# A new order of the same steps in a state read followed by a mixture of attention experts

## The chip, the cores and the metric

One core of a Trainium2 chip runs the whole program. The metric is the device time in microseconds, the median of several executions. The engines are named as in the profile: PE is TensorE (matmuls; PEld are its weight loads), DVE is VectorE, ACT is ScalarE, POOL is GpSimd, SP is SyncE, which issues all DMAs of this kernel.

## What is computed

There are two stages, for 8 batches (B) of 8 heads (H), 512 tokens (S), 32 states (Ns) and 64 features (D). First, tokens read states and states read tokens:

```python
scores = scale * np.matmul(x, state.transpose(0, 1, 3, 2))
a = softmax(scores); xread = np.matmul(a, state)
scores2 = scale * np.matmul(state, x.transpose(0, 1, 3, 2))
a2 = softmax(scores2); sread = np.matmul(a2, x)
x = concat([xread, sread], axis=2)      # then (B, 544, 512)
```

(`softmax` and `concat` stand here for the lines of the reference that spell them out.) Then the 544 rows of each batch, 512 features wide, go through four experts of causal attention with 64 features each. The logits `x @ w_gate` choose two experts for each row; q, k and v are projected by each expert's weights, the masked softmax of q k^T is applied to v, the result goes through the expert's `wo`, and each row's two experts are added with their gate weights. The weights of q and k are 200 times larger than drawn.

## The kernel before

Most products are made in f16 with each operand split in two parts: the high part is a cast to f16, the low part is the f16 of what the cast left over, and three products (high by high, high by low, low by high) are added in PSUM. Batch 0 is done in f32 and batch 1 partly. So nearly every tensor has a step that makes the high part (a cast, on ACT, POOL or DVE) and one that makes the low part (a subtraction, on DVE or POOL).

For each batch b, `front(b)` (line 744; `first`, line 660, for batch 0) loads x into the tile `xn` (one buffer only), splits it into `xh` (`parts_of_x`, line 610), transposes it by DMA into `xT`, makes the scores against the state (`bd`), their softmax in `eb` (`row_softmax`, line 633), its transpose `at`, the weights folded with the state `gs`, and from `at` and `gs` the values `v`, the keys `kt` and the masked queries `qf`, which are split into `qh` and transposed by DMA into `qm`. `side(b)` (line 856) makes the states' own read (`e2`, `a2`, `a2t`, `rd`, `xt_tail`). `gate` (line 881) makes the gate weights in a chain of small DVE and ACT steps. `probs(b, i)` (line 920) makes the attention scores of query tile i (128 rows), their softmax in a `p32` tile (named p in the profile), splits it into `ph` and sends it by DMA transpose to `pt`. `reads(b, i)` (line 990) multiplies `pt` by `v`, scales the result into `z32` (named z), adds its two shared quarters (a step of its own that DVE or POOL can do), splits it into `zh` and transposes it into `z`; `outs` (line 1030) multiplies by `wo_n` and stores `o`. `tail` (line 1045) does the 32 state rows of each pair of batches. `load_wo` (line 568) loads wo in two pieces and splits them into `wo_n` (`hi_lo`, line 446, whose low part is made by `low`, line 433).

Nothing is issued while these functions run: each operation is recorded as a step with a number, its possible engines ("ways") and the buffers that it touches. `Steps.run` (line 346) then issues the 2022 steps in the order of a text written out by hand, `ORDER`. An entry is the step's number, a dot, and the number of the way: for the low part made by `low` way 0 is DVE and way 1 is POOL (two instructions there, a scaling and a subtraction); for an addition on z32 way 0 is POOL and way 1 is DVE; for a cast made by `split` (line 425) way 0 is ACT, 1 is POOL and 2 is DVE. A third number puts that many extra matmuls before the step. So the text sets the order of every engine's queue, SP's queue of DMA issues among them. The dictionary `SLOTS` gives, for each tag with several buffers, which buffer each new use takes, in the order of the text: `bank` are the eight banks of PSUM, for example.

```python
for entry in order:
    s = self.all[int(entry[0])]
    calls = s["ways"][int(entry[1])][2]
    for b in s["bufs"].values():
        if b.slot is None:
            b.slot = self.tags[b.tag][int(next(left[b.tag])) if b.tag in left else 0]
```

All instructions of the steps carry line 362 in the profile, so one tells them apart by tiles. The steps that the prediction names: 265 and 283 are the additions on z32 of two query tiles of batch 0; 266 is a cast of zh; 205 is the low part of the second half of `wo_n`; 589 are the scores of batch 2's x against its state; 398 is a projection of batch 1 (keys, in f32).

Of the kernel before, what the change touches and what calls it, by code (L numbers as in the profile page):

```python
# [125 lines left out]
    "mb": "11000101",  # L126
    "sbm": "01011010",
    "bd": "0101010",
    "m2": "00110010",
    "gs1": "0101010101010",  # L130
    "kt": "010201020",
    "lg": "0100011010010",
# [1076 lines left out]
```

## Time and profile before

| | us |
|---|---|
| median of 3 runs | 285.36 |
| the runs | 285.03, 285.36, 286.33 |
| the profiled execution | 285.13 |
| its span, first to last instruction | 283.1 |
| PE busy in it | 270.6 |
| DVE busy | 240.1 |
| ACT busy | 216.2 |
| POOL busy | 202.6 |
| mean granted clock of TensorE | 0.994 |

The span is 2.0 us shorter than the profiled execution's own time; that rest lies around the first and last instruction. A matmul's end is modelled and matmuls are pipelined, so a high busy share of PE says that matmuls follow one another closely, not that the array is full. The granted clock is a share of 2.4 GHz.

### The profile page before, as it was taken

What the parts mean: (1) busy time and instruction counts of PE and PEld (TensorE: products, weight loads), DVE (VectorE), ACT (ScalarE), POOL (GpSimd) and SP (SyncE); (2) the same over time, 40 slices, a digit from 0 to 9 for tenths busy, and PEclk for the clock granted to TensorE, in tenths of its full rate; (3) what the DMA queues carried; (4) which work ended last, traced back from release to release, by engine and by line L of the source; (5) the groups of instructions that cost most, each with busy time, mean ns of one, the idle gap of its engine ahead of it and who ended that gap; (6) DMA issues with size and microseconds to landing.
All of it is one profiled execution on the core that took longest, in us unless ns stands there. A gap on an engine that the chain in (4) does not pass through costs nothing.

```text
span 283.1 us, 9753 instructions
## 1 busy us (share of the span) xinstructions
PE 270.6 (96%) x3659; PEld 182.7 (65%) x3660; DVE 240.1 (85%) x772; ACT 216.2 (76%) x713; POOL 202.6 (72%) x267
## 2 busy tenths in 40 slices
PE   8997999699999999897999999999999999999994
PEld 4956657277566755677657576776656757676752
DVE  2779999989999999999899989989899768878530
ACT  3768899389897998687989899847996755766643
POOL 7736966689796997866997899967896755438200
PEclk9999999899999999999999999999999999999999
DMA  7959869999999999999999999999957987899845
GB/s 197 186 167 136 215 158 181 239 176 145 195 250 205 191 203 243 200 194 243 205 183 211 182 243 247 229 222 182 133 122 140 153 151 95 134 238 210 158 167 186
DMA packets 154575, 53.20 MB, mean 188 GB/s; under 512 B 140576, under 2 KB 150048, under 8 KB 154528
## 3 DMA queue, kind: packets, MB, share of 16 engines
q1 hardware_dynamic: 154528, 52.59, 97.5%
q8 instruction: 28, 0.46, 0.7%
q14 instruction: 19, 0.16, 0.2%
HBM read 11.02 MB, written 8.91 MB: 70 GB/s over the span
## 4 chain that ended last, share of the span: by engine, by line
PE 60%; DVE 18%; POOL 9%; DMA 5%; issue 3%; ACT 2%; SPq 0%; POOLq 0%; ACTq 0%; DVEq 0%
PE bank L362 60%; DVE xh L362 4%; DMA xn<-in_x_dram 4%; POOL ph L362 2%; POOL eb L362 2%; DVE z L362 2%; DVE bank L362 2%; DMA pt<-ph 1%; POOL qh L362 1%; POOL a L362 1%; DVE v L362 1%; POOL at L362 1%; DVE qh L362 1%; DVE ph L362 1%; DVE qf L362 1%
## 5 line engine op out<-in xcount | busy, mean ns | idle before, releaser
L362 PE MATMUL bank<-gs,at 128*128 128x260 f16 (+3 forms) x352 | 52.3, 294 | 1.7 <-ACT at L362 1.4
L362 PE MATMUL bank<-kt,qm 128*128 128x128 f16 (+13 forms) x368 | 47.7, 313 | 0.0
L362 PE MATMUL bank<-wo_n,z 128*128 128x512 f16 (+1 forms) x198 | 46.1, 373 | 0.0
L362 PE MATMUL bank<-v,pt 128*128 128x192 f16 x480 | 44.1, 246 | 0.8 <-DMA pt<-ph 0.5
L362 PEld LDWEIGHTS <-pt 128*128 128x128 f16 x480 | 40.0, 98 | 4.2 <-DMA pt<-ph 2.3
L362 POOL TENSOR_TENSOR ph<-p,ph 128x256 f16<-128x256 f32 (+3 forms) x25 | 34.0, 1365 | 4.3 <-ACT ph L362 2.4
L362 DVE CUSTOM_DVE_ANT_0 bank<-bank,causal 128x128 f32<-128x128 f32 (+3 forms) x64 | 30.5, 502 | 5.5 <-PE bank L362 4.8
L362 ACT ACTIVATE p<-bank,mx 128x128 f32<-128x128 f32 (+3 forms) x64 | 33.3, 524 | 0.9
L362 PEld LDWEIGHTS <-at 128*128 128x128 f16 x288 | 27.5, 97 | 6.2
L362 PEld LDWEIGHTS <-qm 128*128 128x128 f16 (+1 forms) x336 | 20.2, 96 | 16.0 <-issue 5.6
L362 PEld LDWEIGHTS <-z 128*128 128x128 f16 x198 | 18.8, 98 | 18.1 <-issue 0.7
L362 PE MATMUL bank<-at,gs 128*128 128x512 f16 (+2 forms) x96 | 26.7, 413 | 1.6 <-DVE v L362 1.6
L362 ACT ACTIVATE o<-bank 128x512 f32<-128x512 f32 (+1 forms) x35 | 20.4, 583 | 6.8 <-PE bank L362 6.7
L362 DVE SCALAR_TENSOR_TENSOR xh<-xn,xh 128x512 f16<-128x512 f32 x24 | 20.4, 865 | 5.1 <-ACT xh L362 5.1
L362 ACT ACTIVATE xh<-xn 128x512 f16<-128x512 f32 x32 | 19.3, 624 | 6.2 <-DMA xn<-in_x_dram 6.2
L362 POOL TENSOR_TENSOR zh<-z,zh 128x256 f16<-128x256 f32 x25 | 18.6, 751 | 7.5 <-ACT zh L362 6.3
L362 POOL TENSOR_TENSOR qh<-qf,qh 128x384 f16<-128x384 f32 x21 | 19.9, 956 | 2.5 <-ACT qh L362 2.3
L362 POOL TENSOR_SCALAR ph<-p 128x256 f16<-128x256 f32 (+3 forms) x15 | 12.1, 810 | 12.5 <-ACT p L362 12.3
L362 DVE TENSOR_TENSOR z<-bank,c 128x384 f32<-128x384 f32 x32 | 17.3, 546 | 3.2 <-PE bank L362 2.0
L362 POOL TENSOR_TENSOR a<-e,a 128x512 f16<-128x512 f32 x15 | 18.3, 1223 | 1.0 <-ACT a L362 0.8
L362 POOL TENSOR_TENSOR z<-z 128x128 f32<-128x128 f32 x23 | 10.6, 466 | 10.7 <-DVE z L362 10.4
L362 POOL TENSOR_TENSOR eb<-eb,sbm 128x512 f32<-128x512 f32 x13 | 14.4, 1109 | 5.3 <-DVE sbm L362 5.3
(213 smaller groups left out, 648.6 us busy)
## 6 DMA issues: line engine op xcount, KB each, us to landing
out_dram<-o SPq DMA_DIRECT2D x33, 256.0 KB, 2.8
xn<-in_x_dram SPq DMA_DIRECT2D x14, 512.0 KB, 5.1
xn<-in_x_dram SPq DMA_DIRECT2D x4, 256.0 KB, 3.8
sn<-in_state_dram SPq DMA_DIRECT2D x8, 64.0 KB, 3.6
p<-in_moe_wo_dram SPq DMA_DIRECT2D x2, 256.0 KB, 3.5
xT<-xh SPq DMA_TRANSPOSE x28, 4.0
pt<-ph SPq DMA_TRANSPOSE x25, 4.5
p<-in_moe_wv_dram SPq DMA_DIRECT2D x1, 384.0 KB
```

The source lines that it names most:

```text
L362: f(**{k: v.ap() if isinstance(v, View) else v for k, v in kw.items()})
```

## The change

Only `ORDER` and `SLOTS` differ; the steps and the code that records them stay. All lines of both are replaced. Compared entry by entry, the same 2022 steps stand in both orders. 98 of them have another way:

| from, to | steps |
|---|---|
| ACT to DVE | 18 |
| ACT to POOL | 18 |
| DVE to ACT | 17 |
| DVE to POOL | 18 |
| POOL to ACT | 8 |
| POOL to DVE | 19 |

A step's place in the text moves by 9 places in the mean, by 205 at most (a step of a constant's mask). On TensorE the order of the steps is the same but for some twelve short stretches; of SP's 172 issues 125 can be left in their old order. The two stretches of the text around the steps 265 and 283, in full lines:

```diff
-263.0 786.0 421.0 282.0 264.0 273.0 365.0 369.0 275.0 261.1 581.1 426.0 372.0 360.0 265.1 283.1 21.0 373.0 361.0 376.0 401.0 362.0 366.0 582.0 589.0
-371.0 276.0 380.0 377.0 381.0 378.0 379.0 382.0 204.0 205.1 367.0 278.1 383.0 363.0 384.0 609.0 385.1 597.0 608.0 590.0 610.0 386.0 596.0 284.0 266.0
...
+263.0 281.0 372.0 282.0 366.0 260.0 367.0 585.0 264.0 274.0 273.0 360.0 373.0 362.0 361.0 370.0 369.0 376.0 205.0 261.1 414.0 401.0 581.1 582.0 589.0
+275.0 426.0 265.0 283.0 266.1 276.0 371.0 380.0 377.0 381.0 378.0 363.0 379.0 284.0 382.0 398.0 374.0 609.0 597.0 608.0 590.0 278.1 383.0 596.0 384.0
...
```

Here 261 is the low part of one ph tile (on DVE, way 1, in both), 276 that of a larger one (on POOL in both), 371, 367, 363 and 375 are evictions of the low part of v on DVE, and 277 (in the next line of the text) is the DMA transpose of the ph tile that 276 completes.

The line that holds the load of wo's second half (step 203), and the one with the first half of batch 5's x (1266), before and after:

```diff
-329.1 330.0 422.0 345.0 215.0 233.0 344.0 234.0 346.0 337.1 423.0 235.0 118.0 338.0 240.0 241.0 355.0 356.0 203.0 571.0 218.0 573.0 1053.0 424.0
-816.0 549.0 817.0 903.0 839.0 1062.0 688.0 836.0 489.0 833.0 1266.0 907.0 904.0 831.0 834.0 824.1 703.0 704.0 837.0 825.0 1265.0 493.0 826.0 490.0
...
+321.0 322.0 314.0 197.1 324.0 131.0 318.0 132.0 315.0 84.0 180.0 108.0 81.0 85.0 319.0 325.0 194.0 316.0 207.0 86.0 160.0 137.0 203.0 570.0 88.0
+709.0 718.0 719.0 722.1 552.0 723.0 1074.1 499.0 1266.0 553.0 554.0 725.0 726.0 504.0 710.1 505.0 828.1 829.0 740.0 741.0 711.0 720.0 721.0 1075.0
...
```

`SLOTS` changes with it, tag by tag; three of its lines:

```diff
-    "xh": "3021031203210312",
-    "p32": "12020101010212102110210212001201201002102",
-    "mb": "11000101",
...
+    "xh": "0123013210230123",
+    "p32": "01210202020120120120102102112101120121102",
+    "mb": "01011001",
...
```

## Rows read from the trace of the kernel before

**Rows 1.** Busy us (x instructions) of PE, PEld, DVE, ACT, POOL by stage, clock, DMA
```profile
20.20:57.70 37.50, 33.35 (x394) 21.17 (x396) 35.77 (x117) 30.31 (x102) 26.41 (x30) 0.95 0.90 184
57.70:128.40 70.70, 69.22 (x1036) 46.59 (x1024) 67.61 (x211) 61.11 (x204) 57.91 (x65) 1.00 1.14 201
128.40:278.60 150.20, 148.37 (x2045) 101.25 (x2040) 124.34 (x424) 112.33 (x383) 104.98 (x123) 1.00 0.96 183
```

**Rows 2.** Pieces of the chain that ended last: start us, us, what
```profile
106.59 4.46 DMA xn<-in_x_dram
...
221.50 57.91 PE bank L362 x716
```

**Rows 3.** DVE's timeline, 47.9 to 54.2 us: start, us, engine, line, operation, tiles
```profile
49.43 2.42 DVE L362 TENSOR_TENSOR z<-z 128x128 f32<-128x128 f32 x2
51.77 0.41 DVE L362 SCALAR_TENSOR_TENSOR v<-bank,v 128x256 f16<-128x256 f32 x1
...
53.19 0.41 DVE L362 SCALAR_TENSOR_TENSOR v<-bank,v 128x256 f16<-128x256 f32 x1
```

**Rows 4.** POOL's timeline in the same stretch; in brackets the idle time before
```profile
49.53 2.16 POOL L362 TENSOR_TENSOR ph<-p,ph 128x1024 f16<-128x1024 f32 x1 [0.98 <-ACT bank L362]
```

**Rows 5.** PE's timeline, 43 to 58 us
```profile
51.26 0.84 PE L362 MATMUL bank<-xT,bd 64*32 64x512 f16 x24 [0.87 <-ACT v L362]
53.66 3.18 PE L362 MATMUL bank<-at,gs 128*128 128x512 f32 x4 [1.55 <-DVE v L362]
```

**Rows 6.** Busy times around the half clock, and in another poor stretch
```profile
49.50:54.30 4.80, 2.38 (x31) 1.15 (x30) 4.66 (x14) 1.79 (x9) 2.31 (x2) 1.00 0.95 221
54.30:57.70 3.40, 3.40 (x76) 1.39 (x78) 3.40 (x10) 1.50 (x6) 3.32 (x5) 0.50 1.20 278
21.20:28.30 7.10, 5.48 (x24) 4.51 (x25) 6.89 (x28) 5.95 (x25) 4.57 (x7) 1.00 0.92 136
```

**Rows 7.** Groups by shape: count, busy us, mean ns, idle before
```profile
L362 POOL TENSOR_TENSOR z<-z 128x128 f32<-128x128 f32 x23 | 10.6, 466 | 10.7 <-DVE z L362 10.4 <-DVE gt L362 0.3
L362 DVE TENSOR_TENSOR rd<-bank,s 128x128 f32<-128x128 f32 x8 | 2.2, 279 | 0.7 <-ACT sums L362 0.3 <-PE bank L362 0.2
L362 DVE SCALAR_TENSOR_TENSOR xh<-xn,xh 128x512 f16<-128x512 f32 x24 | 20.4, 865 | 5.1 <-ACT xh L362 5.1
L362 DVE SCALAR_TENSOR_TENSOR gs<-bank,gs 128x512 f16<-128x512 f32 x12 | 8.0, 666 | 0.2 <-ACT gs L362 0.2
L362 DVE SCALAR_TENSOR_TENSOR v<-bank,v 128x256 f16<-128x256 f32 x32 | 13.1, 416 | 0.0
```

**Rows 8.** DVE's timeline, two low parts of xh that took long
```profile
114.49 1.59 DVE L362 SCALAR_TENSOR_TENSOR xh<-xn,xh 128x512 f16<-128x512 f32 x1
...
123.12 2.08 DVE L362 SCALAR_TENSOR_TENSOR xh<-xn,xh 128x512 f16<-128x512 f32 x2
```

**Rows 9.** SP's timeline, the first transposes of x
```profile
21.66 5.81 SPq L362 DMA_TRANSPOSE xT<-xh  x4
```

**Rows 10.** Busy times by stage again, 188 to 218 us
```profile
188.40:203.40 15.00, 15.00 (x222) 10.17 (x220) 14.01 (x40) 11.36 (x35) 12.27 (x15) 1.00 1.08 201
203.40:218.40 15.00, 15.00 (x239) 9.23 (x239) 13.20 (x45) 12.67 (x46) 12.55 (x13) 1.00 0.56 115
```

**Rows 11.** Groups by shape, POOL's casts and subtractions
```profile
L362 POOL TENSOR_SCALAR qh<-qf 128x384 f16<-128x384 f32 x4 | 2.4, 606 | 1.8 <-DVE qf L362 1.8
L362 POOL TENSOR_SCALAR at<-et 128x512 f16<-128x512 f32 x2 | 1.5, 753 | 1.1 <-PE bank L362 1.1
L362 POOL TENSOR_SCALAR ph<-p 128x768 f16<-128x768 f32 x3 | 3.7, 1231 | 5.8 <-ACT p L362 5.8
L362 POOL TENSOR_SCALAR a<-e 128x512 f16<-128x512 f32 x5 | 3.5, 690 | 1.2 <-ACT e L362 1.2
L362 POOL TENSOR_TENSOR qh<-qf,qh 128x384 f16<-128x384 f32 x21 | 19.9, 956 | 2.5 <-ACT qh L362 2.3 <-ACT wgt L362 0.2
L362 POOL TENSOR_TENSOR at<-et,at 128x512 f16<-128x512 f32 x9 | 10.4, 1160 | 3.5 <-ACT at L362 3.4
```

More of the change, by code (lines that the diff above doesn't have):

```diff
@@ L29 @@
 ORDER = """
[89 rows of a table removed]
[89 rows of a table added]
 """
 SLOTS = {
-    "bank": ("012347621350472631417326747026401256017137025702317513265023470126571564150326024176421046021564315025470241027360457602"
-          "431720465237164052341765765403153672410365201647521047251054321576040361245307631275764305712476123406243104505631256147"
-          "20356172461502364752167325016357430261573542650361275643217254675173246012320174662467130175046073157632"),
-    "xh": "3021031203210312",
-    "p32": "12020101010212102110210212001201201002102",
-    "mb": "11000101",
-    "sbm": "01011010",
-    "bd": "0101010",
[L129 to L132, printed above, removed]
-    "s2": "10101010",
-    "gt1": "0111010100011",
-    "a2": "1011101010101010",
-    "gs2": "1010110101001",
-    "gw": "0101110101010",
-    "m6": "11101010",
-    "a2t": "01011101",
-    "qf": "01001001010101101010100110100101",
-    "wgt": "01010101",
-    "qm": "00101101",
-    "mx": "31333212030102310203312031203121",
-    "sums": "01001010",
-    "ph": "0122011202102102011010120",
-    "xt_tail": "0010",
-    "c6": "0011010101010101",
-    "z32": "02100120102010211021210221021120",
-    "zh": "001110101010101",
-    "z": "111010010110101111",
-    "qh": "01101010010110",
-    "o": "1203122023101303213022310102312013",
-    "tw2": "0101",
-    "m4": "0101",
-    "twg": "0101",
-    "tmt": "0101",
-    "tmx": "1100",
-    "tsm": "1101",
-    "tpt": "0100",
-    "tc4": "1000",
-    "tz": "01",
@@ new lines @@
+    "bank": ("210374625103461752672465241531251370236146327623146714760235650341754657652135704257340273240637106426745245027605320176"
+          "451372604715304726410350453214763041273625340172354103721420640735251452067431052411760537142312456051364156757230417612"
+          "54037125627354026135074153076514265173041625740136204563205724507431270362134167002736405132046351205647"),
+    "xh": "0123013210230123",
+    "p32": "01210202020120120120102102112101120121102",
+    "mb": "01011001",
@@ new lines @@
+    "sbm": "00011010",
+    "m2": "01011100",
+    "bd": "0101010",
+    "kt": "012021021",
+    "lg": "0101101000011",
+    "s2": "01010101",
+    "gs1": "0101110101101",
+    "a2": "0101010110100101",
+    "gt1": "1010100000001",
+    "gs2": "1010101101010",
+    "gw": "0101101001001",
+    "a2t": "01011001",
+    "m6": "11101010",
+    "qf": "01010101010110010101010101010110",
+    "qm": "01110011",
+    "wgt": "10110101",
+    "mx": "20133021130102310312031203313210",
+    "sums": "01010101",
@@ L162 @@
+    "ph": "0100120012201202102120120",
+    "xt_tail": "1010",
+    "c6": "0110101010010101",
+    "z32": "12022012011221012102101201200120",
+    "zh": "011010110100101",
+    "z": "010001100101011001",
+    "qh": "10100110010101",
+    "o": "0120323102313212302100132032313012",
+    "tw2": "0100",
+    "m4": "0111",
+    "twg": "1010",
+    "tmt": "1101",
+    "tmx": "1010",
+    "tsm": "0100",
+    "tpt": "0010",
+    "tc4": "0101",
+    "tz": "10",
 }
```

170 rows, old and new, of the table ORDER are left out of this document.

## The prediction

> **What bounds the kernel now.** I read busy time by stage first, then the chain of waits, then the timeline of the place where DVE looks worst, then the groups of instructions by shape. From 128.4 us to 278.6 us TensorE is busy 148.37 of 150.20 us at full clock [rows 1], and the chain's last long piece is 57.91 us of matmuls [rows 2]. Nothing but fewer matmuls would shorten that stage, and the change removes none. So what the change is worth must be earned before 128.4 us, as an earlier start of that stage. In the two stages before it TensorE idles 37.50 - 33.35 = 4.2 us and 70.70 - 69.22 = 1.5 us, and DVE is nearly full: 35.77 of 37.50 us, then 67.61 of 70.70 us [rows 1]. DVE is what the matmuls run against there.
>
> The dearest place is 49 to 58 us. Two DVE additions on the z rows (steps 265 and 283, 128 elements each) take 2.42 us together [rows 3]; an operation of that size with one operand in PSUM takes 0.28 us [rows 7]. In the same time POOL subtracts the low half of a ph tile, from 49.53 to 51.69 us [rows 4], and the second addition ends 0.16 us behind it. So DVE stood still for some 1.9 us (2.42 less twice 0.28). Behind it in DVE's queue are the evictions of v at 51.77 and 53.19 us [rows 3], and the first projection matmul that waits for one (step 398) starts at 53.66 us, released by a DVE v [rows 5]. From 54.30 us the granted clock is 0.50, the 1.2 GHz level, for 3.40 us; before that TensorE was busy 2.38 of 4.80 us [rows 6]. In another poor stretch, 5.48 of 7.10 us, the clock stayed at 1.00 [rows 6].
>
> **The change, part by part.** The diff keeps all 2022 steps; 98 of them change engine, 25 of these before 128.4 us, and the rest is order and buffers.
>
> *The two additions go to POOL* (265.1 and 283.1 become .0). DVE loses 2.42 us. POOL gains two additions of 0.466 us [rows 7] about where it idles 0.98 us before its ph subtraction [rows 4]; that subtraction and the transpose behind it come up to 0.9 us later, which the loads of x that stand ahead of that transpose in SP's queue cover (without them the reads of pt would come 0.9 us later). A cast of zh (step 266) goes to POOL as well, behind the same cover. In exchange the low half of wo_n (step 205) comes to DVE: 0.67 us without a stall, 0.87 us as pieces of that size with both operands in SBUF average [rows 7]. DVE net: 2.42 - 0.67 = 1.75 us earlier. The bounds are 2.4 us (wo_n fits a gap) and -0.9 us (the subtractions of wo_n and ph, which DVE now runs there, wait behind a POOL step as the addition did, up to 2.16 us, and 0.67 us is added). I take 1.75, since POOL's long subtraction stands behind the additions in the new order and DVE's pieces ahead of it.
>
> *TensorE at that place.* Step 398 gets another PSUM bank, whose last reader is the v eviction of 51.77 us and not that of 53.19 us. By DVE's 1.75 us this eviction ends near 50.4 us. What is late next is step 589, the scores, which waits for transposes of x whose place in SP's queue stays: it starts at 51.26 and takes 0.84 us [rows 5] (the trace names ACT as its releaser, long done by then, so I read a transpose). So 398 starts at about 52.1 us, 1.5 us earlier; bounds 0 and 3.2 us. The 3.40 us at half clock did 1.7 us of work: worth 0 or 1.7 us, and with the shorter wait before it I take 1.7. TensorE then leads by 3.2 us at 57.7 us, but DVE only by 1.75, and DVE is the fuller engine from there [rows 1]: the smaller number passes on.
>
> *DVE's other engine changes before 128.4 us.* Between 20 and 50 us a low part of wn and a copy of kt leave DVE, 256 elements each, 0.42 us by the eviction of that size [rows 7], and a few small scalings come: 0.5 us less. Between 57.7 and 128.4 us a subtraction of zh and a cast of a2 leave (some 0.42 us each) and one of qh comes: by the same rows 0.3 us less, or 0.7 us with the stall that zh had; I take 0.5. These lie on a nearly full engine and I count them whole: 1.0 us, bounds 0 and 1.4.
>
> *The other stalls.* A low part of xh, both operands in SBUF, averages 865 ns on DVE; the same operation from PSUM takes 666 ns [rows 7]. So 24 x 0.2 = 4.8 us are lost in the kernel as above, and two places of the full stage show it: 1.59 - 0.67 = 0.9 us, and 2.08 - 1.33 = 0.75 us for a pair [rows 8]. By my count in the order DVE has 62 steps of over 0.3 us with both operands in SBUF before, and 60 after. They may fall better or worse by some 2.5 us, half of the 4.8; I take 0.
>
> The rule behind it: the Trainium skill (SBUF — State Buffer, SBUF: two separate sides) says that a DVE operation with two SBUF inputs and a GpSimd operation that reads SBUF take an exclusive lock on a shared port pair, so that the later one waits for the whole of the other. The 2.42 us agree. The rule also speaks against the change: the low parts of wo_n and ph on DVE would wait whole for the POOL steps that now stand beside them, and by it alone the gain at this place could be nothing; that is the first rival.
>
> *SP's queue.* 47 of its 172 issues change places. The load of wo's second half (step 203, 256 KB) goes ahead of the four transposes of x at 21.66 us [rows 9], where SP is idle before them; at the 184 GB/s of that stage [rows 1] it needs 1.4 us, between the landing of x and those transposes: 0, at worst 1.4 us, and I take 0. Stores of o go ahead of some transposes, and the first half of batch 5's x now goes out right before the second: 0 where SP waits for data anyway, up to 1.5 us (three stores of some 0.5 us) where it does not; I take 0, and the rest stands in the second rival.
>
> *After 128.4 us.* 73 of the engine changes lie here, on engines with slack while TensorE is full: nothing, as long as that slack lasts (the last rival). [...]
>
> **Sum.** 1.75 + 1.0 + 0.2 = 2.95 us, say 3.0. The profiled execution took 285.13 us, 0.23 us under the median of 285.36; against the median this gives 282.4 us, 1.1% faster. A measurement of this kernel can tell about 0.5%, 1.4 us, from no change.
>
> **Rivals.** *The lock forms again* at 49 to 54 us: the 1.75 us are not won, and wo_n's 0.67 us is paid. For it speaks the rule, and POOL's 2.16 us; against it the order, which places DVE's pieces first. Of the rest 1.2 - 0.7 = 0.5 us stays: 284.9 us.
>
> *The lead is eaten between 57.7 and 128.4 us.* The chain goes through a landing of x, 4.46 us from 106.59 us [rows 2]. Both halves of that load now stand together, where one went out earlier, so that 1 MB and not 0.5 MB has to land behind the second, and SP has less slack. Against it: POOL's work ahead of it loses a qh subtraction, 0.956 us [rows 11]. Of the 3.0 us only what lies behind is kept, some 0.7 us: 284.7 us.
>
> *More stalls vanish.* Those of rows 8 and their like do not recur, 2.5 us: 279.9 us. For it: the two come from chance neighbours; against it: as many such steps remain.
>
> *Slower: POOL fills up at 188 to 218 us.* It is busy 12.27 and 12.55 of 15.00 us there [rows 10]. Four casts come to it (qh 0.606, at 0.753 twice, ph 1.231 us), one leaves (a2 0.690), two subtractions come (qh 0.956, at 1.160) and one addition leaves (0.466) [rows 7, 11]: 4.3 us onto 5.2 us of idle time. TensorE gets pt and qm through POOL and SP. It decides from the point at which stalls take the remaining 0.9 us; then TensorE waits up to 4.3 us, and with a stretch at half clock like that above 1.7 us more: 285.36 - 3.0 + 4.3 to 6.0 = 286.7 to 288.4 us. Against it: most of the 4.3 us lies at the end of that stretch, and a transpose that comes late there has to use up TensorE's lead over it first.
>
> **How the numbers follow.** Forecast 0.42 (280.9 to 283.9 us by its own unknowns), more stalls vanish 0.17, lock again 0.10, lead eaten 0.14, POOL 0.17. The range is 278.8 to 287.4 us: it leaves out the far halves of the two outer cases, about 0.17. Faster by over 0.5% (under 283.9 us): 0.41 + 0.17 = 0.58. Within 0.5%: 0.01 + 0.24 x 0.8 = 0.20. Slower (over 286.8 us): the POOL case and what the two middle rivals cost when they come together, 0.17 + 0.05 = 0.22.
>
> **What would show it.** Right: the z additions on POOL at 0.47 us; no half clock near 54 us; the v evictions near 50 us; the stage of full TensorE starting about 3 us earlier and taking 150 us as before. Wrong: a DVE subtraction of 1.5 us or more at 49 to 54 us; a lead at 58 us that is gone by 128 us; TensorE idle for more than 3 us after 128 us; POOL busy over 14.5 of 15 us with SP waiting for it.

## The result: 0.7% slower, and the profile after

The changed kernel takes 288.03 us (median of 14 runs, 286.67 to 288.97) against 285.63 us for the kernel before (14 runs, 284.01 to 287.80): a ratio of 1.0072, 95% interval 1.0046 to 1.0098. The forecast was 282.4 us, 278.8 to 287.4. It lies outside, on the other side of the kernel before.

Busy times of the changed kernel by the stages of [rows 1], same columns (us, busy us of PE, PEld, DVE, ACT, POOL, granted clock, DMA share, GB/s):

```profile
20.20:57.70 37.50, 35.95 (x432) 23.57 (x431) 35.97 (x126) 32.27 (x108) 29.53 (x37) 1.00 0.91 176
57.70:128.40 70.70, 65.69 (x1014) 43.91 (x1014) 64.10 (x201) 59.07 (x197) 56.82 (x63) 1.00 1.11 202
128.40:278.60 150.20, 146.09 (x2017) 99.51 (x2002) 125.31 (x426) 101.64 (x360) 107.35 (x129) 1.00 1.00 180
```

Up to 57.7 us TensorE did more (35.95 us busy, not 33.35), and the half clock is gone. Behind it TensorE, no longer full, idles 5.0 us and 4.1 us, where it idled 1.5 and 1.8 us [rows 1]. DVE is no fuller than before (64.10 of 70.70 us). So TensorE now waits for something else. The table of waits, PE alone, from 57 to 280 us (us in total, times, longest), first of the kernel before:

```profile
PE bank L362 <- DVE qf L362: 1.6, 1, 1.6
PE bank L362 <- DVE kt L362: 0.7, 1, 0.7
PE bank L362 <- DMA pt<-ph: 0.5, 1, 0.5
...
```

and of the changed kernel:

```profile
PE bank L362 <- DMA qm<-qh: 5.1, 5, 1.8
PE bank L362 <- DMA pt<-ph: 2.0, 2, 1.3
PE bank L362 <- issue: 0.9, 1, 0.9
PE bank L362 <- DMA z<-zh: 0.4, 1, 0.4
...
```

That is the result in one view: 9.0 us of waits instead of 3.0, and most of them are for DMA transposes. A second trace of the kernel before, shown below, has 2.0 us of waits for transposes of ph and zh among its 4.3 us; what neither trace of it has is a wait for a transpose of qh. The chain of waits agrees. The chain of the kernel before has no transpose of qh in it, this one has four (start us, us, what):

```profile
62.60 5.84 DMA qm<-qh
99.47 5.46 DMA qm<-qh
152.97 5.59 DMA qm<-qh
243.03 5.44 DMA qm<-qh
```

The place of the prediction's first step, POOL's timeline and then DVE's:

```profile
48.29 1.96 POOL L362 TENSOR_TENSOR z<-z 128x128 f32<-128x128 f32 x2 [1.89 <-DVE z L362]
50.72 2.13 POOL L362 TENSOR_TENSOR ph<-p,ph 128x1024 f16<-128x1024 f32 x1
```

```profile
45.30 1.65 DVE L362 SCALAR_TENSOR_TENSOR wo_n<-p,wo_n 128x512 f16<-128x512 f32 x1
48.14 0.68 DVE L362 SCALAR_TENSOR_TENSOR wo_n<-p,wo_n 128x512 f16<-128x512 f32 x1
48.74 1.20 DVE L362 TENSOR_TENSOR ph<-p,ph 128x768 f16<-128x768 f32 x1
49.87 0.41 DVE L362 SCALAR_TENSOR_TENSOR v<-bank,v 128x256 f16<-128x256 f32 x1
```

DVE no longer stands still for 2.4 us, but two additions on POOL take 1.96 us instead of twice 0.466 [rows 7], and one low part of wo_n takes 1.65 us, where its neighbour takes 0.68.

### The profile page after: what moved, and what is told of

Same layout as the page of the kernel before. It is cut to its first block, busy times and chain, and to the rows that moved or that the text cites. A ratio compares the mean times of both kernels' runs of the same rounds, so it can differ in the third digit from the quotient of the medians.

```text
span 285.8 us, 9744 instructions
## 1 busy us (share of the span) xinstructions
PE 269.1 (94%) x3660; PEld 181.4 (63%) x3660; DVE 237.5 (83%) x774; ACT 207.5 (73%) x693; POOL 206.3 (72%) x277
## 4 chain that ended last, share of the span: by engine, by line
PE 46%; DMA 16%; DVE 14%; POOL 13%; ACT 5%; issue 4%; SPq 1%; POOLq 0%; ACTq 0%; DVEq 0%
PE bank L362 46%; DMA qm<-qh 8%; DMA xn<-in_x_dram 3%; POOL ph L362 3%; POOL xh L362 2%; DMA pt<-ph 2%; DVE xh L362 2%; DVE bank L362 2%; DMA z<-zh 2%; POOL qh L362 2%; POOL xn L362 1%; ACT xh L362 1%; POOL a L362 1%; DMA xT<-xh 1%; DVE v L362 1%
## 5 line engine op out<-in xcount | busy, mean ns | idle before, releaser
L362 PE MATMUL bank<-kt,qm 128*128 128x128 f16 (+13 forms) x368 | 47.9, 313 | 5.1 <-DMA qm<-qh 5.1
L362 POOL TENSOR_TENSOR ph<-p,ph 128x256 f16<-128x256 f32 (+3 forms) x26 | 35.2, 1358 | 3.9 <-DVE ph L362 1.8
L362 PE MATMUL bank<-at,gs 128*128 128x512 f16 (+2 forms) x96 | 26.0, 403 | 1.1 <-ACT e L362 0.7
L362 POOL TENSOR_SCALAR ph<-p 128x256 f16<-128x256 f32 (+3 forms) x18 | 14.4, 799 | 11.4 <-ACT p L362 9.7
L362 DVE SCALAR_TENSOR_TENSOR xh<-xn,xh 128x512 f16<-128x512 f32 x23 | 17.5, 777 | 5.3 <-ACT xh L362 5.2
L362 POOL TENSOR_TENSOR zh<-z,zh 128x256 f16<-128x256 f32 x27 | 17.9, 672 | 4.1 <-ACT zh L362 3.5
L362 POOL TENSOR_TENSOR a<-e,a 128x512 f16<-128x512 f32 x15 | 17.6, 1179 | 2.8 <-ACT a L362 2.7
L362 ACT ACTIVATE gs<-bank 128x260 f16<-128x260 f32 (+4 forms) x32 | 14.4, 476 | 5.9 <-PE bank L362 5.7
L362 POOL TENSOR_TENSOR qh<-qf,qh 128x384 f16<-128x384 f32 x19 | 17.4, 927 | 1.3 <-ACT qh L362 1.1
L362 POOL TENSOR_TENSOR z<-z 128x128 f32<-128x128 f32 x20 | 12.1, 608 | 7.8 <-DVE z L362 7.6
```

The costliest lines, as they stand in the source:

```text
L362: f(**{k: v.ap() if isinstance(v, View) else v for k, v in kw.items()})
```

## The experiments

ORDER and SLOTS can be cut at a step: the entries of one kernel up to it, then the other's, each new use taking the buffer behind the same earlier use. So time can be shared out by stretch. Percentages are against the kernel before, run on the same chip beside each, with 95% intervals. Where the text of the order was written anew, the line of all steps is L352 in the profile.

**First, one local edit, one local undo, and two cuts.** The kernel before with step 1 alone:

```diff
-265.1 283.1
+265.0 283.0
...
-205.1
+205.0
```

> The kernel before with three entries changed: the z additions 265 and 283 on POOL, wo_n's low part 205 on DVE; all else as it was. If the stall behind POOL's subtraction was what cost time at 49 to 52 us (step 1 of the prediction), the scores 589 and the projection 398 start 1 to 1.5 us earlier, the half clock at 54 us is gone, and TensorE leads the kernel before by 1.7 to 3.2 us at 58 us. If the lock forms again with the pieces that now stand there, the lead at 58 us is 0 and the total 285.4 to 286.3 us. Theory S (SP's issue queue, full from 50 to 190 us, lets no lead through): lead 2 to 3 us at 58 us, under 1 us after 160 us, total 284.6 to 285.6 us. Rival (TensorE full after 128 us, a lead stays): total 282.5 to 283.5 us.

Measured: -0.2% (-0.5 to +0.2). That is not told from nothing. Its trace, at a mean granted clock of 0.75, is not used.

The changed kernel with three of SP's issues put back:

```diff
-907.0 688.0
+688.0 907.0
...
+309.0 889.0
...
-1390.0
...
+1171.0 1390.0
```

> The changed kernel with three of SP's issues put back where they were: the transpose of a2 907 behind that of qh 688, the store of o 309 ahead of the transpose of qh 889, the transpose of a2 1390 behind that of qh 1171. Theory S (the lead is lost where transposes of qh wait in SP's queue behind less urgent issues): 688 goes out 1.4 us earlier and 1171 1.9 us earlier, TensorE's waits of 1.9 us at 102 us and 1.5 us at 157 us shrink to under 0.5 us, and the total is 286.0 to 286.7 us against 288.0. Rival (POOL and DVE hand over late, from 157 us on): the waits only change places, total 287.6 to 288.4 us.

Measured: +0.8% (+0.5 to +1.1), no better than the changed kernel. In its trace both named waits are gone, as Theory S has it. But TensorE then waits 1.6 us at 113 us for a transpose of ph and 1.3 us at 177 us for a bank that ScalarE frees when it writes o; the waits only changed places. Both theories were half right.

Two kernels begin as the changed one and go on as the one before, cut at step 405 (57.5 us) and at step 889 (128 us). The joint of the first, against the changed kernel:

```diff
 393.0 402.0 262.0
-405.0 612.0 599.1 431.0 600.0 432.0
+279.0 431.0 432.0 405.0 599.1 410.0
...
```

> The changed kernel's order up to step 405 (57.5 us), then the order, engines and buffers of the kernel before. Theory S: a lead of 3.2 us at 58 us that SP's full queue eats to 0.5 to 2 us by 160 us, and that then stays, for nothing late was changed: total 283.8 to 285.2 us. Rival (only the later engine changes cost time): the lead stays whole, total 282.2 to 282.9 us. Rival (the early changes are worth nothing): 285.4 to 286 us.

> The changed kernel's order up to step 889 (128 us), then that of the kernel before. TensorE leads by 2.0 us there. Theory S: the old issue order has one issue less ahead of 1171, so 1.0 to 2.0 us of the lead stay: total 283.6 to 284.6 us, faster than both kernels. Rival (no lead can pass SP's queue before 160 us): 285.4 to 285.9 us. Rival (all of the loss is made before 128 us): 287 us or more.

Measured: cut at 57.5 us, 283.95 us, -0.5% (-0.8 to -0.2), faster than both kernels and the best of the runs that store all of o. Cut at 128 us, 0.0% (-0.3 to +0.4), as the rival that lets no lead pass has it, and not Theory S. So the new order gains 0.5% up to 57.5 us and loses the same 0.5% from there to 128 us.

**Then the later half, and four candidates for its cause.** The reverse cut at step 889:

```diff
 567.0 995.0 309.0
-889.0 1275.0 1272.0 1104.0
+757.0 889.0 767.0 1275.0
...
```

> The reverse of the last: the order, engines and buffers of the kernel before up to step 889 (130 us), then the changed kernel's. TensorE has no lead at 130 us. Theory W (two losses: the early lead of 2 to 3 us is used up by 160 us at transposes that SP sends late, and the later half of the new order has waits of its own, 0.6 us at 189 us, 1.3 us at 218 us, 0.8 us at 246 us): the first loss cannot occur, the second does, so 0.7 to 1.2% slower than the kernel before, and the waits of TensorE at 147 and 157 us are under 0.5 us each. Rival (the waits at 147 and 157 us are the new half's own and not a lead used up): they stay, 1.5 to 2% slower. Rival (the later half costs nothing by itself): within 0.3% of the kernel before.

Measured: +0.85% (+0.5 to +1.2). The later half costs by itself, as Theory W has it: the waits at 147 and 157 us are gone, but others are in their place, for transposes of z (PE's timeline):

```profile
180.47 2.76 PE L352 MATMUL bank<-wo_n,z 128*128 128x512 f16 x12 [1.49 <-DMA z<-zh]
189.29 1.04 PE L352 MATMUL bank<-wo_n,z 128*128 128x512 f16 x4 [1.13 <-DMA z<-zh]
```

The changed kernel with one TensorE step moved back:

```diff
-1638.0 1437.1
+1638.0 1661.0 1437.1
...
-1640.0 1661.0 1447.0
+1640.0 1447.0
```

> The changed kernel with one TensorE step moved back to its old neighbours: 1661 (96 short matmuls of batch 6's own read) behind 1638, as before, and not between 1446 and 1793; nine PSUM banks change with it. Theory F (three steps of many short instructions stand together there, and TensorE runs out of instructions: nothing in the trace releases it at 218.6 us, and it stands still with its weight loads): the stop of 0.9 to 1.3 us inside step 1798 is gone, the total 0.8 to 1.3 us under that of the changed kernel, or 0.3 to 0.45% slower than the kernel before. Rival (it waited for a bank or for data, and the time is slack): the stop only moves, total as for the changed kernel, 0.6 to 0.8% slower than before.

Measured: +0.6% (+0.3 to +0.9); 0.1% less than the changed kernel, which these intervals can't tell from nothing. What became of the stop stands with its twin below.

The changed kernel with the engines of before behind step 889 (the digits of 73 entries):

```diff
-1760.1
+1760.0
...
-1425.1
+1425.0
...
```

> The changed kernel's order and buffers, but behind step 889 (128 us) each step on the engine that it had in the kernel before: 73 entries. Rival P of the prediction (POOL fills up, its casts and subtractions come late): the waits at 189 and 246 us go, total 0.8 to 2 us less than the changed kernel, 0 to 0.45% slower than before. Theory W with order as its cause (place in the queues, not the engine, makes a transpose late): no gain, 0.5 to 1.2% slower than before; the stop at 218 us stays in both.

Measured: 295.63 us, +4.0% (+3.6 to +4.4). Neither theory had that. The new order needs its new engines behind 128 us; the old order with the new engines was not run.

The changed kernel with stores of o on ScalarE's queue:

```diff
-f = self.nc.sync.dma_start_transpose if transpose else self.nc.sync.dma_start
+f = self.nc.sync.dma_start_transpose if transpose else (self.nc.scalar if isinstance(in_, View) else self.nc.sync).dma_start
```

> The changed kernel with the 36 stores of o issued from ScalarE's queue and not from SP's; nothing else. SP loses some 0.6 us for each, 21 us in all, 13 of them between 57 and 200 us. Theory S (SP's queue of issues is what uses up the lead): the waits for qm and pt at 66, 81, 101, 147 and 157 us shrink from 7 us together to under 3 us, TensorE still leads the kernel before by 2 us or more at 160 us, total 0.2% faster to 0.2% slower than the kernel before. Rival D (the transposes wait for their data from POOL and DVE, or for each other's transfer, and SP only looks full): the waits stay within 1 us of the changed kernel's, total 0.5 to 0.9% slower. Should an issue hold ScalarE as long as it holds SP, ScalarE's evictions come up to 0.6 us later each and the total is over 1% slower.

Measured: +2.3% (+2.0 to +2.7). It answers nothing on SP, for a new wait came in early and TensorE never had the lead to lose: a transpose of z that SP issued at 75.42 us was there only at 85.4 us, and the granted clock is 0.95 from 57.7 to 128.4 us, where the changed kernel's is 1.00. PE's timeline:

```profile
85.40 1.04 PE L352 MATMUL bank<-wo_n,z 128*128 128x512 f16 x2 [3.66 <-DMA z<-zh]
```

Behind that transpose SP's issues of three transposes of pt took 10.8 us, where those of the changed kernel took 9.0 (3.35 and 5.64). That stores on the other queue held them up is not shown.

**Third, the baseline, the bytes, and the last third.** The kernel before, unchanged, for a second trace:

> The kernel before once more, for its trace alone. The run whose first part is the old order, with all its engines and buffers, showed no half clock at 54 us and was 2.6 us ahead of the trace that the prediction rests on, from 54 us on. Theory X (the 3.4 us at half clock and the late start belong to that one execution): here too the clock is 1.00 from 50 to 58 us, the two z additions still take 2.4 us, and step 405 starts 1.5 to 3 us earlier than in the first trace. Rival (the old order brings the half clock, the other run lost it by chance): the clock is 0.50 for some 3 us near 54 us again.

Busy times around 54 us, and the z additions on DVE's timeline:

```profile
49.50:54.30 4.80, 2.68 (x28) 0.98 (x28) 4.66 (x15) 1.58 (x6) 2.26 (x3) 1.00 1.02 257
54.30:57.70 3.40, 3.40 (x104) 2.05 (x104) 3.37 (x12) 2.76 (x10) 3.40 (x5) 1.00 1.03 192
```

```profile
48.23 2.41 DVE L362 TENSOR_TENSOR z<-z 128x128 f32<-128x128 f32 x2
50.57 0.41 DVE L362 SCALAR_TENSOR_TENSOR v<-bank,v 128x256 f16<-128x256 f32 x1
```

In this trace it is as Theory X has it: the 2.41 us are there, the half clock of [rows 6] is not, and from 54 us on TensorE is some 2.5 us ahead of the first trace. But the half clock does not belong to that one execution. The old order of steps up to 58 us is in seven traces of this study, and the half clock in two of them (the other is the run with the new order of issues, below). And of the 95 executions of the kernel before that ran beside the experiments, 39 have a mean granted clock of 0.994, that of the first trace, or less; they took some 1.1 us longer than the others on the same chip. None of the changed kernel's 14 is below 0.997. Where in those 39 the low clock lay is not on record: with the new first part and the old rest, 6 of 24 executions have 0.994 too. In one of the others, that of the kernel before with cut stores below, TensorE did the same work before that place as in [rows 6], and the clock stayed at 1.00:

```profile
49.50:54.30 4.80, 2.38 (x31) 1.22 (x30) 4.66 (x14) 1.78 (x9) 2.17 (x1) 1.00 0.98 230
```

Both kernels with a quarter of each store:

```diff
-st.dma(to, o, 0.73, par=(1.28, 8, 0.6))
+st.dma(to[:, :P], o[:, :P], 0.73, par=(1.28, 8, 0.6))
```

> The changed kernel, but each full store of o writes 128 of its 512 columns, so three quarters of those rows stay unwritten: some 6 MB and about 7% of the transfers' time less, the same number of issues on SP. To be read beside the run of the kernel before with the same cut. Theory D (from 57 to 190 us the transfers themselves are full, 1.1 of the 16 engines' time, and transposes that PE waits for stand in that stream): waits for qm, pt and z shrink and this kernel gains more than the kernel before does, the two differ by under 0.35%. Rival W (the later half's order has waits of its own, on POOL, DVE and PE's instructions): both gain alike, 0.6 to 0.9% between them stay.

> The kernel before with the same cut of its stores of o (128 of 512 columns written). Both theories: TensorE has little to win, its waits after 58 us are 3 to 4 us in all and mostly on DVE; the last store lands earlier by under 1 us: total 0 to 0.5% faster than the kernel before.

Measured: the changed kernel -0.25% (-0.5 to 0.0), the kernel before -0.65% (-0.9 to -0.4). Between them 0.4% stay of 0.7%, and the waits for qm at 102 and 157 us are still 1.2 and 1.6 us long in the changed one. It falls between the forecasts of D and W: the load of the transfers may have a share in the loss, but it doesn't explain those waits.

The old order up to step 1372 (192 us), the new one behind it:

```diff
 1770.0 1587.0
-1372.0 1247.0 1657.0
+1581.1 1763.0 1781.0 1372.0 1247.0 1657.0
...
```

> The order, engines and buffers of the kernel before up to step 1372 (192 us), then the changed kernel's. With the same cut at 130 us the time was 0.85% over that of the kernel before, and its trace lost 3 us between 160 and 192 us and 1.3 us behind it. Theory D (loss where transfers are full, before 192 us): 0.2 to 0.5% slower, from the stop at 218 us and the wait for qm at 246 us alone. Rival (the loss is the last third's own): 0.7 to 0.9% slower.

Measured: +0.4% (+0.1 to +0.6), within D's forecast. By the cuts, then, the new order is worth about -0.5% up to 58 us, +0.5% to 128 us, +0.5% to 192 us (0.85 - 0.37) and +0.4% behind: +0.9%, against 0.72% measured on the whole. Each of the four rests on intervals of 0.2 to 0.35% to either side.

**Last, SP's order alone, both ways.** All 172 issues of SP take the order of the other kernel; nothing else moves on its own queue, and no buffer follows another one than it did. The changed kernel with the old order of issues, then the kernel before with the new one, at one place of some hundred:

```diff
-683.0 703.0 704.0 502.0 1062.0 907.0 688.0 816.0
+687.0 683.0 688.0 1266.0 907.0 703.0 704.0 502.0 816.0
...
```

```diff
-1062.0 688.0 836.0 489.0 833.0 1266.0 907.0
+683.0 687.0 688.0 502.0
...
```

> The changed kernel with the whole order of SP's 172 issues as in the kernel before; the order and engines of all other steps, and which buffer follows which, stay as changed. Theory S2 (from 58 to 192 us it is the order of SP's issues that makes transposes late): the waits for qm, pt and z between 58 and 192 us shrink from 8 us to under 4 us and the total is 0.5 to 1.0% less than the changed kernel's: 0.3% faster to 0.2% slower than the kernel before. Rival E (the order and engines of the steps that make the data): within 0.25% of the changed kernel, 0.5 to 1.0% slower than before.

> The reverse: the kernel before with the whole order of SP's issues of the changed one, all else as before. Theory S2: 0.4 to 1.0% slower than the kernel before, with waits for qm at 100 and 156 us. Rival E: within 0.25% of it.

Measured: +3.3% (+2.7 to +3.9) and +2.1% (+1.6 to +2.6). The second is the clearest run of the study. SP's timeline of the kernel before, of the changed one, and of the one before with the new order of issues:

```profile
96.31 1.47 SPq L362 DMA_TRANSPOSE qm<-qh  x1
97.87 1.68 SPq L362 DMA_TRANSPOSE xT<-xh  x1
99.64 1.51 SPq L362 DMA_TRANSPOSE qm<-qh  x1
```

```profile
94.85 1.44 SPq L362 DMA_TRANSPOSE qm<-qh  x1
96.38 1.60 SPq L362 DMA_TRANSPOSE xT<-xh  x1
98.04 1.33 SPq L362 DMA_TRANSPOSE a2t<-a  x1
99.47 1.49 SPq L362 DMA_TRANSPOSE qm<-qh  x1
```

```profile
95.22 2.32 SPq L352 DMA_TRANSPOSE qm<-qh  x1
97.63 1.66 SPq L352 DMA_TRANSPOSE xT<-xh  x1
99.33 1.33 SPq L352 DMA_TRANSPOSE a2t<-a  x1
100.75 1.48 SPq L352 DMA_TRANSPOSE qm<-qh  x1
```

A transpose of a (step 907) that TensorE needs only at 110 us stands ahead of the second transpose of qh. On PE's timeline, in the same two kernels, the attention scores (step 725) wait for it:

```profile
104.98 3.36 PE L362 MATMUL bank<-kt,qm 128*128 128x384 f16 x22 [1.76 <-DMA qm<-qh]
```

```profile
106.26 1.96 PE L352 MATMUL bank<-kt,qm 128*128 128x384 f16 x14 [1.76 <-DMA qm<-qh]
```

The wait is 1.76 us in both, and in both the matmuls start 5.51 us after the issue. The kernel before has no such wait. The new order of issues also brings it those at the places of 157 and 246 us (1.35 and 0.91 us). These three waits are therefore brought by SP's order, not by the engines that make the data. For S2 against E this is decisive as to where these waits of qm come from.

The length of the issue that moved ahead is not all of it. At 157 us the kernel before and the changed one issue the transpose at the same time, with a transpose of a on either side in both:

```profile
152.98 1.49 SPq L362 DMA_TRANSPOSE qm<-qh  x1
```

```profile
152.97 1.48 SPq L362 DMA_TRANSPOSE qm<-qh  x1
```

Yet it lands 3.8 us after its issue in the kernel before and 5.6 us in the changed one. So it is at all three places: 3.8 to 3.9 us in the kernel before, 5.4 to 5.6 us in the changed one and in the one before with the new order of issues. In each of these six late transfers the traffic all but stops for about a microsecond, while one packet of 16 KB moves on queue 8, which the profile calls instruction; in the kernel before this stop comes behind the landing, or at its very end. The traffic of the kernel before from 150 to 160 us, in 40 slices of 0.25 us, and that of the changed one (it stops from 158.25 and from 156.75 us):

```profile
GB/s 279 290 290 288 253 238 215 217 219 198 196 189 224 221 210 171 121 206 217 208 218 221 197 193 204 223 215 210 178 124 206 254 117 0 0 5 10 9 150 290
```

```profile
GB/s 232 215 222 216 172 229 228 214 209 205 161 153 220 210 210 164 124 226 219 208 214 223 190 191 172 212 230 54 0 0 7 9 9 182 291 276 287 294 291 286
```

So the order of issues decides also which transfer such a stop falls into. That the packet is what makes a transpose late is inferred from the two coming together; no run moves these packets alone.

As to the total, S2 against E is not decided: the old order of issues takes those at 102 and 157 us out of the changed kernel (TensorE is 1.7 us earlier than there at 160 us, 0.5 of it from before 58 us), and then it stops for 4.12 us, for a bank that ScalarE frees when it writes o:

```profile
188.67 1.57 PE L352 MATMUL bank<-v,pt 128*128 128x192 f16 x11 [4.12 <-ACT o L352]
```

ACT's timeline shows why: its step on o waits for a store of o, which in the old order of issues comes too late for the new order's use of o's buffers.

```profile
188.02 0.60 ACT L352 ACTIVATE o<-bank 128x512 f32<-128x512 f32 x1 [5.25 <-DMA out_dram<-o]
```

Behind this stop the granted clock is 0.96 from 190 to 220 us. Order of issues and order of steps fit each other; half of either in the other costs 2 to 3%.

The last third with step 1661 moved back (the edit of the run above):

> The run with the old order up to 192 us and the changed kernel's behind it (0.37% slower than before, a stop of 1.0 us inside TensorE's step 1798 at 217 us and a wait for qm of 0.6 us at 245 us), with TensorE's step 1661 moved back behind 1638. Theory F (three steps of many short instructions in a row stop TensorE there): the stop is under 0.4 us and the total 0 to 0.2% slower than the kernel before. Rival: the stop only moves, 0.3 to 0.5% slower.

Measured: +0.4% (0.0 to +0.8), no gain over the same kernel without the move. The stop itself is gone. PE's timeline of the changed kernel, then of this one:

```profile
216.38 1.12 PE L362 MATMUL bank<-xh,a2t 128*32 128x64 f16 x96
217.43 1.15 PE L362 MATMUL bank<-wn,bd 64*32 64x512 f16 x41
219.52 0.30 PE L362 MATMUL bank<-wn,bd 64*32 64x260 f16 x7 [0.93 <-issue]
```

```profile
216.17 0.84 PE L352 MATMUL bank<-wn,bd 64*32 64x512 f16 x24
217.35 0.53 PE L352 MATMUL bank<-wn,bd 64*32 64x260 f16 x24 [0.34 <-DVE qf L352]
```

With 96 short matmuls right ahead, PE stops within the 48 of the next two steps, for nothing that the profile shows. Without them it doesn't, and waits 0.34 us for DVE's qf. So Theory F holds for the stop, and the rival for the total.

## Why the prediction was wrong, step by step

**The first part was costed from one execution.** "The 3.40 us at half clock did 1.7 us of work: worth 0 or 1.7 us, ... I take 1.7." They are absent from five of seven traces of that part, and by the clocks on record a low clock comes in some two executions of five and costs about 1.1 us there, wherever it lies: at most some 0.5 us on average. Step 398 starts at 51.05 us in the changed kernel, earlier than the 52.1 forecast, but at 52.30 to 53.87 us in the seven traces, of which [rows 5] is a late one. At the last marker before 58 us (the product with ident and rd, 56.65 us in the changed kernel) TensorE leads the seven by 0.5 to 3.2 us, 1.65 in the median. So the 3.2 us forecast there came true against the trace that it was worked out from, and only half of it against the others; the 1.75 us that went into the sum were near this, for another reason.

**Step 1, DVE 1.75 us earlier: right in kind, too large.** The additions moved and the half clock isn't there. The v eviction starts at 49.87 us, 1.9 us ahead of the first trace's 51.77 [rows 3] and 0.7 us ahead of the second trace's 50.57. The stall moved more than it vanished: wo_n's other low part takes 1.65 us at 45.30 us, and ph's 1.20 us where it took 0.94. POOL pays too: the two additions take 1.96 us there, beside DVE's two SBUF pieces, instead of the 0.93 assumed, that is 0.98 us each instead of 0.466 [rows 7]. The Trainium skill (SBUF — State Buffer, SBUF: two separate sides) lets whichever engine starts first have the shared ports for its whole operation, so that the other one waits, be it DVE or GpSimd; the long additions agree. Against the 2.25 us that the sum has up to there (1.75, and 0.5 of DVE's other changes), the cut at 57.5 us measured 0.5%, about 1.4 us. DVE's other changes can't be seen by themselves.

**SP's queue, "I take 0": the step that failed.** I bounded it at 1.5 us and looked only at stores and loads; I counted 47 moved issues and did not ask, for each transpose of qh, what had come to stand ahead of it and when it would land. With all else as before, the new order of SP's issues by itself costs 2.1%, some 6 us, and brings the three waits for qm; in the changed kernel these are 1.76, 1.37 and 0.64 us. The cuts put the loss from 58 to 192 us at 1.0%, 2.8 us. The first two of the waits lie in that stretch, but the total is not their sum: with three issues put back they are gone, and nothing is gained. The other waits there aren't traced to one move; the first wait for qm, 1.05 us at 67 us, is not SP's, for that issue ends 0.04 us behind DVE's last step on qh, at 65.08 us.

From 57 to 190 us SP's issues fill 120 of 133 us in either kernel (summed over its timeline). That is an upper bound of SP's own work, since some issues, like the one just named, last until their data is there. With each issue at the shortest of its kind in the trace it would be 84 us in the kernel before and 82 us in the changed one. So the queue is busy, but how much slack it has isn't known.

**"After 128.4 us ... nothing": wrong.** I read TensorE's 148.37 of 150.20 us as saturation, that is as slack on all other engines. It says only that this order let everything arrive in time. In the changed kernel the same 150.20 us hold 146.09 us of matmuls. The wait at 157 us is SP's order, the stop at 218 us is TensorE's own order. The 0.2 us that the sum adds to its two other terms are shown by no run; in this stage TensorE idled 4.1 us where it had idled 1.8.

**The rivals.** "The lead is eaten between 57.7 and 128.4 us" (0.14) came true in its stretch, by transposes of qh and ph and not by the landing of x. "The lock forms again" (0.10) came on POOL's side, with 1.96 us for the two additions, while DVE won 0.7 to 1.9 us. "More stalls vanish" (0.17) came in kind: a low part of xh takes 777 ns on DVE and not 865, some 2 us in all, and the total gained nothing from it. "POOL fills up at 188 to 218 us" (0.17) gave 286.7 to 288.4 us, and 288.03 lies in it, but the mechanism isn't this one. POOL there, busy times (fifth engine figure):

```profile
188.40:203.40 15.00, 14.56 (x217) 9.59 (x215) 13.95 (x38) 9.36 (x28) 12.03 (x15) 1.00 1.09 195
203.40:218.40 15.00, 15.00 (x234) 9.73 (x232) 13.15 (x48) 11.21 (x44) 14.26 (x15) 1.00 0.59 107
```

It rose to 14.26 us in one half only, under the 14.5 that I had named, and TensorE lost 0.44 us in the 30 us. The old engines put back made it worse by 3.3%. A right total, then, for a wrong reason.

**The signs named in advance.** TensorE idle for over 3 us behind 128 us came (4.1 us), and part of the lead was gone by 128 us; a DVE subtraction of 1.5 us at 49 to 54 us did not come. Of the signs of being right, the v eviction near 50 us came and no half clock near 54 us; the additions on POOL took 0.98 us and not 0.47, and the last stage did not start 3 us earlier.

**What stays open.** Which moves cost the rest from 108 to 192 us, where the waits change places when one is taken out; what share the load of the transfers has; and whether the packets on queue 8 make transposes late.

## What to carry to other kernels

Before a step of a tuned order is costed from one trace, look at a second trace of the same kernel, and at the granted clock of its other executions: a stretch at half clock that comes in some executions only is worth its cost times their share. Where one queue issues all transfers, treat it as an engine: list for each transfer that the bounding engine waits for when it is issued, what has come to stand ahead of it, and how long it takes to land, in both traces. A bounding engine at 99% busy is a property of the order that feeds it, and so a new order can lose there even where it removes no slack that a view of busy times shows.

## What the runs showed of the hardware

- TensorE's clock: with the same busy share before it (2.38 of 4.80 us) the granted clock fell to 0.50, the 1.2 GHz level, in one execution of the kernel before and stayed at 1.00 in another with cut stores.
- TensorE can stop for nothing that the profile names: 0.69 to 0.93 us of "issue" at the same matmul (after 40 or 41 of 48), in two orders whose first parts differ. Queue 8, which the profile calls instruction, moves 0.46 MB in 28 packets over the run, which would be 63 bytes for each of TensorE's 7,320 instructions; two of the packets came within 4 us around this stop in the changed kernel. That TensorE waits there for its own instructions is an inference.
- A DMA transpose landed late where such a packet of 16 KB moved beside it. Of the changed kernel's 88 transposes with a known landing, 23 had one that started from 0.5 us before to 1.3 us after the end of their issue; these landed 3.4 us after that end on average, the other 65 2.4 us. In the kernel before it is 3.5 us (11) against 2.4 us (66).
- An operation of 128 x 128 with both operands in SBUF took 0.98 us each on POOL beside such operations on DVE, and 0.466 us on average on POOL in the kernel before.
